# Other places in SBUF for the loads of the later retention, and another order of the steps, in a fused retention and SwiGLU kernel

## Chip, cores and metric

One core of a Trainium2 chip. The metric is the device time of one execution in microseconds (us); lower is better. "Span" is the stretch that the profiler shows of one execution, from its first instruction to its last.

## The reference

Retention with a decay per head is followed by a SwiGLU block. With batch 4, 8 heads, 768 positions and 64 numbers per head:

```python
for t in range(S):
    state = gamma[None, :, None, None] * state + np.einsum('bhd,bhe->bhde', k[:, :, t], v[:, :, t])
    y[:, :, t] = scale * np.einsum('bhd,bhde->bhe', q[:, :, t], state)
x = np.ascontiguousarray(y.transpose(0, 2, 1, 3)).reshape(B * S, H * D)   # 3072 x 512
g = x @ w_gate                                                             # 512 x 1536
silu = g * (1.0 / (1.0 + np.exp(-g)))
out = (silu * (x @ w_val)) @ w_out                                         # 1536 x 512
```

## The kernel before

The 3072 tokens are worked off in four segments of 6 x 128 tokens, 0 to 3. Each segment has a retention, which gives x; a pass up (gate and value products, silu, the product of both, giving h, kept in the tile `hT`, one row of 768 numbers per block `f` of 128 of the 1536 columns); and a pass down (h times `w_out`). The retention of segment s+1 is mixed into the end of the pass up and into the pass down of segment s, so that TensorE (PE) has work of the one while the other waits for vector work. Numbers are split in three parts before they meet PE (first part on ScalarE, ACT; second on VectorE, DVE; third on GpSimd, POOL, or on DVE).

Nothing schedules the program but a string, `PLAN`, of 2345 steps. The steps are recorded one by one in that order; each engine takes its own instructions in that order and waits at each for its operands and for its place to come free. So a step that waits holds up all that stands behind it on its engine. All loads and stores but a few go through one engine's queue, SP, and wait there in the same way: a load whose place is still being read holds up every later load.

Steps of segment s stand as `s/name`; those of the first pass up have no `s/`. The ones used below:

- `l0` to `l14` (`load_pair`): loads of the retention, 512 KB each; five for each of three pairs of chunks p: k and q turned (`l0 l1`, `l5 l6`, `l10 l11`, one DMA, L789), then v, k by rows, and q by rows (`l2 l3 l4`, `l7 l8 l9`, `l12 l13 l14`, four DMAs each, L793). The tuple `HOME` names for each load one of the `homes`, stretches of 1024 numbers per partition.
- `scp` scores on PE, `decp.i` decay on DVE (they free banks 4 to 7), `qp.c` scaling of q on DVE, `kp.n` scaling of k on ACT (L831), `Ap` and `Bp` the two halves of the mixing on PE (L798), `newp.z` the state on DVE (L897), `wasp.zg` and `mvp.z` on ACT (L889, L844), `yp.zr` y out of PSUM on ACT (L1025), `sum` and `x` the making of x (L414, L1003, L1010).
- `pf.n`: one of seven products of block f of a pass up (six matmuls, L1091). `uf.n`: silu and sums of that block on ACT and DVE. `wf.g.0`, `.1`, `.2`: the split of its weights (L994, L997, then L1000 on POOL or L414 on DVE; the set `ELSE` names those on DVE). `Lf` (`load_unit`, L1063): load of those weights, 896 KB, into `loads`, in which homes 0 to 4 lie too.
- `Df.t`: one step of a pass down (three matmuls, L1160), block f, 128 tokens t. `hf.0` to `.2`: split of row f of h. `Wf` (L1139; L1136 in segment 0): load of block f of `w_out`, 768 KB, into one of three slots; it waits until the last D of the block three before is done. In segment 0 it is 256 KB and is split by `df.0` to `.2` (ACT L1003, POOL or DVE, DVE), and `Zf` (L1150) stores the result.
- `et`, `ot`: result of tokens t out of PSUM into `chunk_x`, and its store (L1197). `Gf:i`, `Wf:i`, `if:i`, `jf:i`: the first pass up (PE, PE, ACT, DVE). `S`, `C`, `Z` of a number over 11: `w_out` as it is made in the first pass up.

Of the kernel before, what the change touches and what calls it, by code (L numbers as in the profile page):

```python
# [1331 lines left out]
```

## Time and profile before

| | us |
|---|---|
| three executions | 660.14, 662.2, 663.5 |
| median | 662.2 |
| the profiled execution | 666.25 |
| its span | 664.1 |

The page of the profile gives busy times by engine over the span and in 40 slices; the chain of waits follows the work that ended last back from the end; the timeline gives instructions of an engine in order of time, with the idle time before each in brackets and what ended it; the table by windows gives busy times and the granted clock of PE in chosen stretches. In the timeline "x33" is 33 instructions in a row that were merged. SPq is the SP queue; its column of time is the time to issue, not to land.

### The profile page before, as it was taken

The page shows a single profiled execution, that of the slowest core. Times are in us where ns is not written, and L with a number is a line of the kernel's source. Part 1 is how long each engine was busy: PE and PEld are TensorE (multiplying, and loading weights), DVE is VectorE, ACT ScalarE, POOL GpSimd, SP SyncE. Part 2 cuts the span into 40 slices and gives each one's busy share as a digit, 9 for nine tenths or more (in the row PEclk, how much of TensorE's full clock was granted, in tenths as well). Part 3 has the DMA queues.
Part 4 walks back from the last instruction along what each step waited for, and adds up shares of the span by engine and source line. Part 5 has one row for each costly group of instructions (what it writes and reads, how often), then busy time and mean ns, then how long its engine had stood idle before and what let it go on. Part 6 is the DMA issues. An engine that isn't in the chain of part 4 may idle for free.

```text
span 664.1 us, 14143 instructions
## 1 busy us (share of the span) xinstructions
PE 642.2 (97%) x5587; PEld 589.1 (89%) x5587; DVE 495.2 (75%) x760; ACT 391.7 (59%) x815; POOL 183.8 (28%) x122
## 2 busy tenths in 40 slices
PE   8999999998989989999999999999889999999997
PEld 7999989886869979998878999999678899999886
DVE  3988687867989947787689778787678788777541
ACT  3778788966655656556667665546474465554221
POOL 1442545420112745520000514520000524452000
PEclk9999999997999979999999999999899999999999
DMA  9899987897986651456884724446976643403564
GB/s 314 275 353 302 373 275 256 301 321 305 319 282 217 226 157 57 154 192 210 281 308 170 255 77 167 143 147 199 287 230 229 212 153 128 167 0 100 199 220 148
DMA packets 60850, 144.59 MB, mean 218 GB/s; under 512 B 5872, under 2 KB 33008, under 8 KB 60784
## 3 DMA queue, kind: packets, MB, share of 16 engines
q1 hardware_dynamic: 60208, 142.90, 63.3%
q8 instruction: 44, 0.72, 0.4%
q10 hardware_dynamic: 576, 0.79, 0.4%
q14 instruction: 22, 0.18, 0.1%
HBM read 113.78 MB, written 29.88 MB: 216 GB/s over the span
## 4 chain that ended last, share of the span: by engine, by line
PE 58%; DMA 4%; ACT 1%; SPq 0%; issue 0%; DVE 0%; ACTq 0%
PE bank L1091 35%; PE bank L1160 19%; DMA oitem<-wdnt 3%; PE bank L798 3%; DMA loads<-in_k_n_dram 0%; SPq L793 0%; ACT loads L831 0%; ACT states L889 0%; ACT gitem L994 0%; DVE chunk_x L1183 0%; ACT tmp L1106 0%; ACT bank L1107 0%; ACT chunk_x L1185 0%; ACT bank L1110 0%; ACT xb L1003 0%
## 5 line engine op out<-in xcount | busy, mean ns | idle before, releaser
L1160 PE MATMUL bank<-oitem,gitem 128*128 128x512 f32 x867 | 209.0, 398 | 6.2 <-DMA oitem<-wdnt 4.6
L1160 PEld LDWEIGHTS bank<-oitem,gitem 128*128 128x128 f32 x867 | 163.0, 191 | 43.0 <-DMA oitem<-wdnt 2.4
L1091 PE MATMUL bank<-xa,gitem 128*128 128x384 f32 x864 | 159.9, 339 | 3.3 <-ACT tmp L1106 3.3
L1091 PEld LDWEIGHTS bank<-xa,gitem 128*128 128x128 f32 x864 | 152.9, 191 | 4.0 <-ACT tmp L1106 3.6
L1000 POOL TENSOR_TENSOR gitem<-gitem 128x768 fp32r<-128x768 f32 x48 | 96.3, 2016 | 175.1 <-DVE gitem L997 154.0
L1000 POOL TENSOR_TENSOR oitem<-oitem 128x256 fp32r<-128x256 f32 (+1 forms) x51 | 56.1, 1103 | 167.8 <-DVE oitem L997 149.8
L922 PE MATMUL bank<-xa,oitem 128*128 128x384 f32 x480 | 85.3, 336 | 2.1 <-DVE hT L459 1.1
L922 PEld LDWEIGHTS bank<-xa,oitem 128*128 128x128 f32 x480 | 82.9, 188 | 3.6 <-DVE hT L459 1.8
L997 DVE SCALAR_TENSOR_TENSOR gitem<-gitem,loads 128x768 fp32r<-128x768 f32 x72 | 75.9, 1069 | 11.4 <-ACT gitem L994 11.3
L1091 PE MATMUL bank<-xb,gitem 128*128 128x384 f32 x432 | 81.8, 335 | 0.0
L994 ACT ACTIVATE gitem<-loads 128x768 fp32r<-128x768 f32 x72 | 58.8, 841 | 34.8 <-PE bank L1091 26.2
L1091 PEld LDWEIGHTS bank<-xb,gitem 128*128 128x128 f32 x432 | 75.8, 188 | 0.2
L414 DVE SCALAR_TENSOR_TENSOR gitem<-gitem 128x768 fp32r<-128x768 f32 x72 | 71.2, 994 | 1.9
L997 DVE SCALAR_TENSOR_TENSOR gitem<-gitem,hT 128x768 fp32r<-128x768 f32 x48 | 46.0, 962 | 23.3 <-ACT gitem L994 23.2
L994 ACT ACTIVATE gitem<-hT 128x768 fp32r<-128x768 f32 x48 | 39.9, 840 | 36.8 <-PE bank L1160 29.6
L1091 PE MATMUL bank<-xb,oitem 128*128 128x384 f32 x216 | 43.8, 337 | 0.0
L1108 DVE TENSOR_TENSOR hT<-bank,tmp 128x384 f32<-128x384 f32 x36 | 20.0, 555 | 30.6 <-PE bank L1091 29.9
L1107 ACT COPY tmp<-bank 128x384 f32<-128x384 f32 x36 | 17.2, 477 | 36.0 <-PE bank L1091 20.1
L1091 PEld LDWEIGHTS bank<-xb,oitem 128*128 128x128 f32 x216 | 38.0, 188 | 0.2
L889 ACT ACTIVATE states<-states,local 128x64 f32<-128x64 f32 x120 | 31.5, 335 | 1.5 <-DVE states L897 1.5
L1025 ACT COPY chunk_x<-bank 128x256 f32<-128x256 f32 x36 | 12.4, 367 | 30.4 <-DVE states L897 16.1
L1108 ACT COPY tmp<-bank 128x384 f32<-128x384 f32 x36 | 17.3, 480 | 14.1 <-PE bank L1091 14.0
(125 smaller groups left out, 786.2 us busy)
## 6 DMA issues: line engine op xcount, KB each, us to landing
loads<-wup SPq DMA_DIRECT2D x36, 896.0 KB, 5.0
oitem<-wdnt SPq DMA_DIRECT2D x33, 768.0 KB, 5.2
wdnt<-oitem SPq DMA_DIRECT2D x12, 768.0 KB, 5.3
wup<-first SPq DMA_DIRECT2D x9, 896.0 KB, 6.4
rawp<-in_w_gate_dram SPq DMA_DIRECT2D x12, 512.0 KB, 7.4
rawp<-in_w_val_dram SPq DMA_DIRECT2D x12, 512.0 KB, 6.5
rawp<-in_w_out_dram SPq DMA_DIRECT2D x12, 512.0 KB, 7.1
out_dram<-chunk_x SPq DMA_DIRECT2D x21, 256.0 KB, 2.3
```

Of the source, the lines that this page charges most:

```text
L414: stt(o, x, 1.0, y, op0=mul, op1=op)
L798: nc.tensor.matmul(o, a, b, start=start, stop=True, skip_group_check=True)
L889: act(states[:, z, g, n], states[:, 1 - z, g, n], AF.Copy, scale=lg[:, ds(NP * g + n, 1)])
L922: nc.tensor.matmul(o, w[:, a, ts(b, P)], X0[:, a, i, NC - 1 - b], start=a == b == 0, stop=a == 2 and b == NC - 1, skip_group_check=True)
L994: act(o[0], x, AF.Copy, scale=CUT / FAR)
L997: stt(o[1], f32(o[0]), -FAR, x, op0=mul, op1=add)
L1000: op(o[2], f32(o[0]), f32(o[1]), op=add)
L1025: copy(cx[:, ds(2 * r, 2), :, half[z]], y)
L1091: nc.tensor.matmul(o, w[:, a, k], x[:, a, KH - 1 - k], start=start and a == k == 0, stop=a == 2 and k == KH - 1, skip_group_check=True)
L1107: lambda: act(gate, c11, AF.Silu, scale=ONE), lambda: copy(u2, x),
L1108: lambda: copy(p5, wb), lambda: tt(h1, x, p5, op=add),
L1160: nc.tensor.matmul(banks[tok][:, cols], hs[f][:, a, ds(i * TH + u * P, P)], wo[f][:, a, cols], start=f == a == 0, stop=f == NF - 1 and a = ...
```

## The change

Before, the fifteen loads of a retention share seven homes: five in `loads`, the upper half of `chunk_x` and the second quarter of `tmp`. After, there are twelve: four more in the first 4096 numbers of `hT` (rows 0 to 5 of h, which are free once `h0` to `h5` have read them) and the lower half of `chunk_x` (free when the stores of the results of tokens 0, 1, 4 and 5 are done, and written by y later).

| load | before | after |
|---|---|---|
| l0, l1 (k, q of pair 0) | loads 2, loads 3 | chunk_x low, loads 2 |
| l2, l3, l4 | loads 4, chunk_x high, loads 2 | loads 3, chunk_x high, loads 4 |
| l5, l6 (pair 1) | loads 0, loads 1 | loads 2, chunk_x low |
| l7, l8, l9 | loads 3, tmp, loads 0 | tmp, hT 1, hT 0 |
| l10, l11 (pair 2) | loads 1, loads 4 | loads 0, loads 1 |
| l12, l13, l14 | chunk_x high, loads 0, loads 1 | hT 2, hT 3, chunk_x high |

The same 2345 steps are recorded, in another order from the 151st on, and `ELSE` has 50 names, not 45. In segment 0, `d0.1` and `e4` move to DVE and `d9.1` to POOL. Of the third parts of the weights of the passes up of segments 1, 2 and 3, 8, 13 and 12 stand on DVE before and 11, 11 and 16 after (the others on POOL); new on DVE in segment 1 are `w2.0.2`, `w2.1.2`, `w6.0.2`, `w7.2.2` and `w10.1.2`. Of the order, only the stretches that the prediction speaks of are shown.

```diff
     homes = [loads[:, ts(i, 1024)] for i in range(5)]
     homes += [chunk_x[:, ts(1, 1024)], tmp[:, ts(1, 1024)]]
-    HOME = (2, 3, 4, 5, 2, 0, 1, 3, 6, 0, 1, 4, 5, 0, 1)
+    homes += [hT.rearrange("p f i t -> p (f i t)")[:, ts(i, 1024)] for i in range(4)]
+    homes += [chunk_x[:, ts(0, 1024)]]
+    HOME = (11, 2, 3, 5, 4, 2, 11, 6, 8, 7, 0, 1, 9, 10, 5)
     blocks = [loads[:, ds(i, UNIT)] for i in (2048, 2048 + UNIT, 0)]
     lmask = local[:, : NP * HC].rearrange("p (i n) -> p i n", i=2)
...
-    G11:1 a17 b17 0/h1.0 1/k0.1 1/k0.3 0/W0 0/W1 j10:1 S17 c17 C17 0/h0.2
-    1/q0.1 1/was0.01 0/h1.1 j10:0 W11:0 i11:0 i11:1 1/l5 1/l6 0/d0.0 0/d0.1 j11:0 0/h1.2
-    Z17 0/h2.0 0/h4.0 0/d1.0 1/was0.00 0/d0.2 W11:1 0/W2 0/d1.1 j11:1 T10:1 0/Z0 1/A0
-    0/D0.0 0/d1.2 0/h2.1 0/D0.1 0/D0.2 1/sc1 1/l8 1/new0.0 0/h2.2 0/Z1 1/y0.00 0/d2.0 0/d2.1
-    1/mv0.0 1/dec1.1 1/dec1.0 1/was0.11 0/D0.3 0/D1.0 0/D0.4 0/D0.5 0/h3.0 1/l9 0/d2.2 0/Z2 1/k1.3
-    T9:2 T10:2 0/h4.1 0/D1.2 0/D1.3 0/D1.5 0/D1.1 0/h4.2 1/was0.10 1/y0.01 0/D1.4 1/k1.2 1/q1.0
-    0/h5.0 0/W3 0/d3.0 0/d3.1 1/k1.1 0/h3.1 1/q1.1 1/B0 0/D2.0 0/D2.1 0/D2.2 Z10 Z9
-    0/W4 1/begin 1/new0.1 0/d3.2 0/h5.1 0/h3.2 1/y0.10 1/y0.11 1/k1.0 1/mv0.1 0/D2.5 1/A1 0/D3.0
...
-    1/p2.3 1/u2.3 1/p2.4 1/w2.2.2 1/u2.4 0/e3 1/w3.2.1 1/w3.0.2 1/p2.5 1/u1.2 0/o3 1/u2.5 1/p2.6
-    1/L6 1/u0.7 1/u2.6 1/w4.1.0 1/w4.0.0 1/w4.2.1 1/w3.2.2 1/p3.0 1/w4.0.1 1/u2.8 2/l3 1/w5.2.0 1/w4.2.2
-    1/p3.1 1/w4.1.1 1/w4.0.2 1/u3.0 1/p3.2 1/u3.1 1/L7 1/p3.3 1/u3.3 1/u2.2 1/u2.7 1/p3.4 1/u3.4
-    1/w4.1.2 2/k0.3 1/u1.7 1/p3.5 1/w5.1.0 1/w5.0.0 1/u3.5 1/u2.9 1/p3.6 1/w6.2.0 1/w5.2.1 1/w5.2.2 0/e5
...
-    1/D5.5 1/D4.4 1/D5.0 1/D5.4 2/l13 2/y1.11 2/was1.11 2/y1.10 2/sum1.2 2/x1.1.0 2/new1.1 2/mv1.1 1/D5.3
-    2/L0 1/W7 1/D5.2 1/D6.0 2/sc2 2/x1.1.2 2/sum1.0 2/sum1.1 2/sum1.3 1/W8 1/h7.0 1/h7.1 1/h7.2
...
-    2/h1.1 2/u11.3 2/u11.2 2/u11.4 2/p11.4 2/u11.5 3/l8 2/p11.5 2/h2.0 2/h1.2 2/D0.0 2/u11.6 2/D0.2
-    2/p11.6 3/begin 2/u11.7 2/h2.1 2/u11.8 2/h4.0 2/u11.9 2/D0.1 2/D0.3 2/D1.0 3/k1.3 3/k1.1 3/k1.2
-    3/k1.0 2/h2.2 2/h4.1 2/h4.2 3/A0 3/new0.0 3/was0.10 3/sc1 3/y0.01 3/y0.00 2/D1.3 2/D1.1 3/l9
-    2/W2 3/was0.11 3/dec1.1 2/D1.2 3/mv0.0 3/dec1.0 2/D0.4 2/D0.5 2/D1.5 2/W3 2/h3.0 3/B0 3/y0.10
...
-    2/h5.1 2/h5.2 2/h6.1 2/D4.1 2/D3.0 2/W6 3/A1 3/new1.0 3/x0.0.1 2/h6.2 2/D4.0 3/y1.00 3/y1.01
-    2/D4.2 2/D4.3 3/mv1.0 3/was1.10 3/was1.11 3/B1 3/l13 3/new1.1 3/y1.10 3/y1.11 3/x0.0.2 3/sum1.0 3/sum1.1
-    3/sum1.3 2/D4.4 2/D4.5 3/L0 2/W7 2/h7.0 3/sc2 3/was2.01 3/x1.2.0 3/x1.2.1 3/dec2.0 2/h7.1 3/k2.3
...
+    c17 0/h1.0 1/k0.1 i11:0 G11:1 i11:1 0/W0 1/k0.3 0/d0.0 1/cm j10:1 0/h0.2 1/q0.0
+    Z11 1/q0.1 0/W1 j10:0 W11:0 S17 C17 0/h1.1 1/l9 1/was0.01 0/h1.2 W11:1 Z17
+    0/h2.0 0/d1.0 0/h4.0 1/was0.00 0/W2 j11:0 j11:1 1/l7 0/d0.1 0/d0.2 0/Z0 1/A0 0/h2.1
+    1/new0.0 T10:1 1/mv0.0 1/l8 0/D0.0 1/sc1 0/D0.1 1/y0.00 0/d2.0 0/d1.1 0/d2.1 0/d1.2 0/Z1
+    1/was0.11 0/D0.3 0/D0.2 0/D1.1 0/D1.0 1/dec1.1 1/dec1.0 0/D0.4 0/D0.5 0/D1.2 0/D1.3 0/h3.0 0/d2.2
+    0/Z2 0/h4.1 T9:2 T10:2 0/h2.2 0/D1.5 1/y0.01 1/k1.3 0/W3 1/B0 0/D1.4 0/D2.2 1/k1.2
+    1/was0.10 1/q1.0 0/h5.0 0/d3.0 0/h3.1 Z10 0/h4.2 1/new0.1 1/q1.1 0/D2.0 0/D2.1 Z9 0/W4
+    1/begin 0/h5.1 0/d3.1 0/d3.2 1/l10 0/Z3 0/h3.2 1/y0.10 1/y0.11 1/k1.1 1/mv0.1 0/D2.3 1/k1.0
+    1/A1 0/D3.0 1/x0.1.0 0/d4.0 1/was1.00 1/x0.1.2 1/sum0.0 1/sum0.1 1/l12 0/D2.5 0/D2.4 0/h6.0 0/W5
...
+    1/u0.9 1/p2.1 1/p2.0 1/w2.1.1 1/w2.2.1 1/w2.2.2 0/e3 0/o3 0/o1 1/L5 1/u1.4 1/w3.1.0 1/w3.1.1
+    2/l3 1/u1.5 1/w2.1.2 1/p1.5 1/w3.0.0 1/u2.0 1/w3.2.0 1/u1.6 1/w1.2.2 1/p1.6 1/u1.8 1/w4.2.0 1/w3.2.1
+    1/u2.1 1/w3.1.2 1/p2.2 1/w3.0.1 1/u1.9 1/p2.3 1/u2.3 1/p2.4 1/u2.4 1/p2.5 1/w3.0.2 1/w3.2.2 1/u1.2
+    1/u2.5 1/p2.6 1/L6 1/u2.6 1/w4.2.1 1/w4.1.0 1/w4.0.0 1/w4.1.1 1/w4.0.1 1/w4.0.2 1/p3.0 1/u2.8 1/w5.2.0
+    1/p3.1 1/u3.0 1/p3.2 1/u0.7 1/L7 1/p3.3 1/u3.3 1/u2.2 1/u2.7 1/p3.4 1/u3.4 1/w4.1.2 1/w4.2.2
+    2/k0.3 1/u1.7 1/p3.5 1/w5.1.0 1/w5.0.0 1/u3.5 1/p3.6 1/u2.9 1/u3.8 1/w6.2.0 1/w5.2.1 1/w5.2.2 0/e5
...
+    1/u11.5 2/q0.1 1/w11.2.2 1/p11.6 2/begin 1/u11.6 1/u11.7 1/h2.1 2/l8 1/W2 1/D0.1 1/D0.3 1/D0.0
+    1/u11.8 1/u11.9 2/A0 2/sc1 2/y0.00 2/k1.1 1/h2.2 2/l10 1/h4.1 2/l7 1/D1.0 1/D1.3 1/D0.2
+    2/k1.0 2/y0.01 2/k1.3 2/dec1.0 2/dec1.1 1/h4.2 1/D0.4 1/D0.5 1/W3 1/D1.5 1/h3.0 1/D1.1 1/D1.2
+    1/D1.4 1/W4 1/h5.0 2/new0.0 2/mv0.0 1/h3.1 2/q1.0 1/D2.1 1/D2.5 2/was0.10 2/k1.2 2/B0 2/L0
+    1/D2.2 1/D2.4 2/q1.1 1/h5.1 2/was0.11 2/y0.11 2/new0.1 2/mv0.1 1/h3.2 1/h5.2 2/was1.00 2/was1.01 2/y0.10
+    2/x0.2.0 2/sum0.2 2/sum0.0 2/sum0.1 2/x0.1.0 2/x0.1.1 2/sum0.3 2/x0.2.1 2/x0.1.2 1/D2.0 1/D2.3 1/W5 1/h6.0
+    1/h6.1 1/h6.2 2/l12 2/x0.0.0 2/l13 1/D3.3 1/D3.2 1/D4.3 1/D3.5 2/L1 1/D3.4 1/D3.1 1/D3.0
+    1/W6 2/x0.0.2 2/A1 2/y1.00 2/new1.0 2/was1.10 2/x0.2.2 1/D4.1 2/x0.0.1 2/y1.01 1/D5.1 1/D4.0 1/D4.5
...
+    2/p11.1 3/q0.0 3/q0.1 2/u10.6 2/u9.7 2/h1.1 2/h0.1 3/l9 2/u11.1 2/u10.9 2/p11.2 2/u10.7 2/p11.3
+    2/u11.3 2/p11.4 2/u11.2 2/u11.4 2/p11.5 2/h2.0 2/h0.2 2/u11.5 3/l7 2/h1.2 2/p11.6 2/u11.8 2/D0.0
+    2/D1.0 2/u11.6 2/u11.7 2/D0.2 3/begin 2/h4.0 2/u11.9 2/h2.1 3/l8 2/D0.3 3/k1.2 3/k1.1 2/h2.2
+    3/sc1 2/h4.1 2/h4.2 3/dec1.0 3/A0 3/new0.0 3/y0.01 3/y0.00 3/was0.10 2/D0.1 2/D1.1 2/D1.3 3/mv0.0
+    3/k1.0 3/was0.11 3/dec1.1 2/D0.4 2/D0.5 2/h3.0 2/D1.2 2/h3.1 3/q1.0 2/h3.2 2/D1.5 2/W2 2/W3
+    2/D1.4 2/W4 2/h5.0 3/B0 3/k1.3 3/y0.10 3/l12 2/D2.3 2/D2.0 3/l10 2/D2.1 2/D2.2 2/D2.4
...
+    3/x0.1.2 3/x0.2.2 3/was1.01 3/sum0.0 3/sum0.1 3/mv0.1 2/D3.2 3/A1 3/was1.00 3/new1.0 3/x0.2.1 3/sum0.3 2/h5.1
+    3/L0 3/l13 2/h5.2 2/D3.3 2/D4.2 2/D3.0 2/W6 2/D4.0 2/D4.1 3/y1.00 2/h6.0 3/y1.01 3/x0.0.0
+    3/mv1.0 3/B1 3/was1.11 3/was1.10 3/new1.1 2/h6.1 2/h6.2 3/y1.10 3/y1.11 2/D4.4 3/x0.0.1 3/x0.0.2 3/sum1.0
+    3/x1.2.0 3/x1.2.2 3/sum1.1 3/was2.01 2/D4.5 2/D4.3 2/W7 3/was2.00 3/k2.0 2/D5.2 2/D5.1 2/D5.0 2/D5.3
+    3/sc2 2/D5.4 2/D5.5 3/k2.1 2/h7.0 2/h8.0 2/h7.1 2/h8.1 3/x1.1.0 2/h9.0 3/dec2.0 3/sum1.3 3/k2.2
```

## The prediction

> **What bounds the kernel now.** I read the page first: the span and the busy times.
>
> ```profile
> span 664.1 us, 14143 instructions
> PE 642.2 (97%) x5587; PEld 589.1 (89%) x5587; DVE 495.2 (75%) x760; ACT 391.7 (59%) x815; POOL 183.8 (28%) x122
> ```
>
> PE is the bound, and the change gives it no instruction more or fewer. What can move is its idle time, 664.1 - 642.2 = 21.9 us with both ends, and time that it runs at a lower clock. So the timeline of PE comes next, for each place in the span at which PE stood, then the windows around the longest.
>
> ```profile
> 132.10 4.43 PE L922 MATMUL bank<-xa,oitem 128*128 128x384 f32 x24 [1.12 <-DVE hT L459]
> 154.98 0.90 PE L798 MATMUL bank<-tmp,loads 64*64 64x64 f32 x29 [1.89 <-ACT chunk_x L1025]
> 195.90 0.96 PE L798 MATMUL bank<-tab,chunk_x 64*64 64x64 f32 x29 [1.30 <-DVE states L897]
> 242.40 7.04 PE L1091 MATMUL bank<-xa,gitem 128*128 128x384 f32 x24 [3.31 <-ACT tmp L1106]
> 252.40 4.33 PE L1091 MATMUL bank<-xa,gitem 128*128 128x384 f32 x24
> 340.52 5.04 PE L1160 MATMUL bank<-oitem,gitem 128*128 128x512 f32 x21 [1.20 <-ACT states L889]
> 469.86 10.72 PE L1160 MATMUL bank<-oitem,gitem 128*128 128x512 f32 x39 [1.99 <-DMA oitem<-wdnt]
> 488.58 7.77 PE L1160 MATMUL bank<-oitem,gitem 128*128 128x512 f32 x33
> 498.31 3.00 PE L1160 MATMUL bank<-oitem,gitem 128*128 128x512 f32 x12 [1.96 <-DMA oitem<-wdnt]
> 517.37 6.40 PE L1160 MATMUL bank<-oitem,gitem 128*128 128x512 f32 x27 [0.69 <-DMA oitem<-wdnt]
> ```
>
> The bracket is PE's idle time. Equal rows give the price of the clock: 24 matmuls took 7.04 after the wait of 3.31 and 4.33 ten microseconds later, 2.7 more; 39 down matmuls took 10.72 after the wait of 1.99, where 33 took 7.77, that is 39 in 9.2, so 1.5 more. In the table by windows the last three figures are PE's clock, the DMA share and GB/s:
>
> ```profile
> 153.00:163.00 10.00, 7.93 (x108) 6.38 (x108) 5.93 (x12) 7.41 (x22) 1.26 (x1) 0.66 0.70 282
> 239.00:249.00 10.00, 6.69 (x24) 6.61 (x24) 3.28 (x6) 6.63 (x17) 4.19 (x2) 0.66 0.27 105
> 467.00:477.00 10.00, 8.01 (x27) 6.20 (x28) 8.09 (x16) 7.25 (x17) 0.00 (x0) 0.83 1.00 310
> 496.00:506.00 10.00, 8.04 (x135) 6.09 (x136) 8.67 (x12) 4.90 (x10) 0.00 (x0) 1.00 0.89 283
> ```
>
> After the waits of 1.89, 3.31 and 1.99 the clock fell, by 3.4, 3.4 and 1.7 us of full-clock work in ten; after that of 1.96 it did not. A wait near 2 us may thus cost itself or nearly twice itself. The Trainium skill ("TensorE: Matmul & The Clock Gate", Part 1 and the goals under "Why this matters for your kernels") states that the clock halves after an idle window of about 3.4 us, that the window runs freely, and that gaps up to about 3 us are safe. This trace disagrees on the last: 1.89 and 1.99 were enough. By the page's rule only the wait of 3.31 has a clock price, and the sum below would be 1.5 us smaller.
>
> **Part by part.** From the rows above a D step is 7.77 / 11 = 0.71 us and a product 4.33 / 4 = 1.08; scores and mixing come from these rows (64 and 96 matmuls). The distances below are counted in `PLAN` with these four prices.
>
> ```profile
> 140.41 1.16 PE L798 MATMUL bank<-loads 64*64 64x64 f32 x64
> 328.74 1.56 PE bank L798 x96
> ```
>
> *Pass up 1, the wait of 3.31.* ACT waits here for l3:
>
> ```profile
> 228.53 2.97 SPq L793 DMA_DIRECT2D chunk_x<-in_k_n_dram  x4
> 237.69 0.40 ACT L831 ACTIVATE chunk_x<-chunk_x,local 128x128 f32<-128x128 f32 x1 [3.33 <-DMA chunk_x<-in_k_n_dram]
> 238.98 0.40 ACT L831 ACTIVATE chunk_x<-chunk_x,local 128x128 f32<-128x128 f32 x1 [0.89 <-DMA chunk_x<-in_k_n_dram]
> ```
>
> From the first issue, 228.53, to the second half's arrival, 238.98, are 10.5 us. `PLAN` puts four products (p3.1 to p3.4, 4.3 us) between `2/l3` and `2/k0.3`; silu and sums queue behind k0.3, and PE runs dry. After, twelve stand there (p1.5 to p3.4, 13.0 us), and l3 still stands right behind `o3`. 13.0 covers 10.5, so the wait and its slow matmuls go: -3.3 - 2.7 = -6.0. What would be late next on ACT is work for products a unit further on.
>
> *Pass down 2, the waits of 1.99 and 1.96.* The queue of SP:
>
> ```profile
> 461.03 2.73 SPq L793 DMA_DIRECT2D loads<-in_q_t_dram  x4
> 463.86 5.95 DMA oitem<-wdnt
> 488.19 0.54 SPq L1063 DMA_DIRECT2D loads<-wup  x1
> 488.82 9.35 DMA oitem<-wdnt
> 510.60 6.64 DMA oitem<-wdnt
> oitem<-wdnt SPq DMA_DIRECT2D x33, 768.0 KB, 5.2
> ```
>
> Here `3/l9` wanted the home of l5, held until sc1; its four issues (2.73) stood ahead of W2, which landed 5.95 after its issue and 2 us late. After, l9 and l7 issue well before; ahead of W2 stands l8, held by `h2.1`. From there to D2.1 PE has nine D steps, sc1, A0 and B0: 6.4 + 1.2 + 3.1 = 10.7 against 2.7 + 6.0 = 8.7. The wait goes with its clock: -3.5. W7 landed after 9.35 because l13 and L0 (896 KB) went out just before it, all held by B1. After, L0 needs only B0 and l13 only `h5.1`: both stand ahead of W6, eight D steps and B1 (7.2) before W7, which then has twelve D steps and sc2 (9.7) to land, against the usual 5.2: -2.0. W10 keeps its eight D steps (5.7 against 6.64), so the 0.69 stays.
>
> *Pass down 1, the wait of 1.20.* In the chain of waits, the way to this one runs from l13 (home of l9, held by B1) over the scaling of k on ACT to PE. After, l13 is in `hT`, held by `h5.1`, some 18 us of PE ahead of k2.1: -1.2.
>
> *Pass down 0.* W11:0 waited 1.12 for `j10:0`, on DVE behind `S17` and `h1.1`; after, both stand behind it: -1.1. But `d0.1`, now DVE's, and `d0.2` stand behind `j11:1`, which can't start before the last matmul ahead of A0 is done. These rows stand for the three:
>
> ```profile
> L459 DVE TENSOR_TENSOR hT<-bank,tmp 128x384 f32<-128x384 f32 x20 | 10.9, 551 | 6.2 <-ACT tmp L459 3.7 <-PE bank L922 2.5
> L1010 DVE SCALAR_TENSOR_TENSOR oitem<-oitem 128x512 fp32r<-128x512 f32 x12 | 8.2, 686 | 5.4 <-POOL oitem L1006 5.3
> ```
>
> 0.55 + 2 x 0.69 = 1.9 with some 0.2 of latency, against 1.56 of A0, then D0.0 needs them: +0.6. The wait of 1.89 at A1 came from W3 by way of d3.0 and y0.1:
>
> ```profile
> 142.89 3.50 SPq L793 DMA_DIRECT2D loads<-in_q_t_dram  x4
> 147.12 0.38 SPq L1136 DMA_DIRECT2D oitem<-wdn  x1
> 153.46 0.63 ACT L1003 ACTIVATE oitem<-oitem 128x512 fp32r<-128x512 f32 x1 [3.87 <-DMA oitem<-wdn]
> ```
>
> W3 stands behind Z2, so behind d2.0 to d2.2, so behind the landing of W2. After, l9's four issues (3.50 as here) stand ahead of W2, and I put W2 1.3 late; against that W3 to A1 holds one D step more (0.7), a scaling of k has left ACT's queue ahead of y0.1 (0.7), and D0.0 already lost 0.6. 1.89 + 1.3 - 0.7 - 0.7 - 0.6 = 1.2, between 0 and 4: I leave this wait and its clock as they are, 0. The 1.30 at B2 and the smaller ones stay too: DVE is as loaded in this stretch as before.
>
> *New waits.* In passes 1 and 2, l8 now waits for `h2.1`, and k1.1 or k1.2 on ACT for l8; two y, one was and mv0.0 queue behind, and B0 needs them.
>
> ```profile
> loads<-in_k_n_dram SPq DMA_DIRECT2D x12, 128.0 KB, 2.9
> L831 ACT ACTIVATE chunk_x<-chunk_x,local 128x128 f32<-128x128 f32 x24 | 8.1, 392 | 4.7 <-DMA chunk_x<-in_k_n_dram 4.7
> L889 ACT ACTIVATE states<-states,local 128x64 f32<-128x64 f32 x120 | 31.5, 335 | 1.5 <-DVE states L897 1.5
> L1025 ACT COPY chunk_x<-bank 128x256 f32<-128x256 f32 x36 | 12.4, 367 | 30.4 <-DVE states L897 16.1 <-PE bank L798 12.9 <-DVE xb L414 1.3
> ```
>
> Issue and landing 2.7 + 2.9; on ACT two k of two instructions (1.6), two y (0.7), a was of four at 31.5 / 120 (1.1) and mv0.0, taken like two y (0.7): 9.7 from `h2.1` to B0, where PE has nine D steps, sc1 and A0, 9.2. So 0.5 late in each pass: +1.0. In pass 1, W2 has 0.4 to spare (twelve D steps, A0 and sc1, 11.2, against the end of h2.1, 2.1 after p11.6, and 8.7), and W5, queued behind L0, has eight D steps and A1 (7.2) against 5.2 to 9.35, so 0 to 2.1 late: +0.5. Nothing that reads a home was seen late for the two loads in `chunk_x` low; if the cover of o5 went, l0 has 37 us in pass 1. Moved DMAs are the same bytes; passes 3 and the first up are taken as before.
>
> Sum: -6.0 - 3.5 - 2.0 - 1.2 - 1.1 + 0.6 + 1.0 + 0.5 = -11.7, from the profiled execution's 666.25 (span 664.1 and 2.15 outside) to 654.5. That execution lies 4.05 over the median of 662.2, so an ordinary one may hold one slow-clock stretch less, and there is about 2 less to win: 662.2 - 11.7 + 2 = 652.5.
>
> **Rivals.** *Slower: DVE bounds pass up 1.* Today's first half of that pass:
>
> ```profile
> 208.00:239.00 31.00, 31.00 (x179) 30.77 (x178) 24.71 (x39) 15.77 (x33) 19.88 (x12) 1.00 0.63 196
> L414 DVE SCALAR_TENSOR_TENSOR gitem<-gitem 128x768 fp32r<-128x768 f32 x72 | 71.2, 994 | 1.9
> L414 DVE SCALAR_TENSOR_TENSOR xa<-xa,tmp 128x1024 fp32r<-128x1024 f32 x9 | 11.0, 1218 | 0.0
> ```
>
> DVE (third busy figure) has 24.7 of 31. After, w2.0.2 and w2.1.2 (2.0), x2.0.1 (1.2), now behind p0.0, and e4 (0.7, as the 128x512 above) come on top: 28.6, and 2.4 of idle are left for its waits, not 6.3. If it needs the 20% that it has now, 28.6 becomes 35.9, 4.9 late, and another such loss in the second half, where w6.0.2 and w7.2.2 join; broken into four waits over 2 us with a slow clock of 1.7 each, 9.8 + 6.8 over 652.5 is 669. It decides once DVE needs more than 2.4. Against it: weights are split a unit ahead.
>
> *Given back.* The four-part loads in front of W2 and W5 in pass 1, or of W3 in pass 0, cost two waits of 2 with 2.5 of clock each: 652.5 + 9 = 661.5.
>
> *The homes do not decide.* W loads wait for their slots anyway, and new holds (`h2.1`, `h5.1`) take the place of B0 and B1; only pass up 1 and W11:0 improve: 662.2 - 7.1 + 2.1 = 657.
>
> *More than forecast.* The wait at A1 goes as well, with 3.4 of clock, and no new ones come: 652.5 - 1.9 - 3.4 - 1.5 = 645.7.
>
> **How the numbers follow.** Forecast 0.54, more 0.10, homes do not decide 0.14, given back 0.13, slower 0.09. Differences under 0.5% (3.3 us: under 658.9 is faster, over 665.5 slower) a measurement of this kernel can hardly tell from none. Faster 0.54 + 0.10 + 0.14 = 0.78; same 0.13; slower 0.09. The forecast's own spread, from the waits at A1 (0 to 4) and W5 (0 to 2.1) and the clock, is some 5 to each side; the range reaches past "more" to 644 and past "given back" to 663, leaving out the slower case and some of the tails.
>
> **What the profile after would show.** Right: no wait for `in_k_n` on L831 in pass up 1 and no slow clock there; no PE wait on `oitem<-wdnt` over 1 us in pass 2; l9 and L0 issued earlier; the wait at A1 still there; 0.7 at W10. Wrong: waits of 2 us on DVE's hT lines in pass up 1; W2 or W5 late in pass 1; more than three slow-clock stretches.

## The result and the profile after

| | executions (us) | median | ratio to before | profiled execution | its span |
|---|---|---|---|---|---|
| before | 657.98 to 663.5 (5) | 660.14 | | 666.25 | 664.1 |
| after | 648.92 to 653.76 (5) | 650.1 | 0.9851, 95% [0.9803, 0.9899] | 648.92 | 647.1 |

The executions of before are those taken beside the changed kernel; with the ratio, the 662.2 of the prediction becomes 652.3 (649.2 to 655.5 by the interval), where 652.5 was forecast. The way there was partly another one. The page of after, its span, its busy times and the line of PE's clock in 40 slices:

```profile
span 647.1 us, 14096 instructions
PE 633.4 (98%) x5587; PEld 581.1 (90%) x5587; DVE 503.2 (78%) x763; ACT 392.8 (61%) x817; POOL 184.2 (28%) x117
PEclk9999999999999999999999999999999999999999
```

The same 5587 matmuls are busy 8.8 us less: no slice is below full clock. The other 8.2 of the 17.0 us between the two spans were idle time. The timeline of PE in after, at the places the prediction named (the bracket is the idle time before the row):

```profile
153.25 0.90 PE L801 MATMUL bank<-tmp 64*64 64x64 f32 x29 [0.67 <-ACT chunk_x L1028]
166.73 0.63 PE L801 MATMUL bank<-tmp 64*64 64x64 f32 x27 [1.02 <-ACT chunk_x L1028]
235.54 4.32 PE L1094 MATMUL bank<-xa,gitem 128*128 128x384 f32 x24
317.56 2.79 PE L1163 MATMUL bank<-oitem,gitem 128*128 128x512 f32 x11 [0.67 <-DMA oitem<-wdnt]
500.48 6.37 PE L1163 MATMUL bank<-oitem,gitem 128*128 128x512 f32 x27 [0.26 <-DMA oitem<-wdnt]
```

A1 of pass down 0 waits 0.67, not 1.89. Pass up 1 has no wait: 24 matmuls take 4.32 where they took 7.04. W10 in pass down 2 is 0.26 late, not 0.69. New are 1.02 at B1 and 0.67 at W5 of pass down 1. The same four windows as before (the last three figures are PE's clock, the DMA share and GB/s):

```profile
150.00:160.00 10.00, 9.02 (x124) 7.08 (x123) 5.24 (x9) 5.16 (x13) 1.27 (x1) 1.00 0.99 386
239.00:249.00 10.00, 10.00 (x59) 10.00 (x59) 8.79 (x15) 6.43 (x12) 3.62 (x2) 1.00 0.52 203
467.00:477.00 10.00, 10.00 (x192) 8.10 (x191) 7.33 (x11) 8.83 (x28) 0.00 (x0) 1.00 1.04 348
496.00:506.00 10.00, 9.74 (x43) 7.79 (x42) 8.27 (x11) 3.69 (x7) 1.83 (x1) 1.00 0.50 152
```

The stretch around A1 now runs at full clock (0.66 before), which was not forecast. Last the groups by line. First the down matmuls, before and after (busy time, mean ns of one, then idle time ahead of them and its releasers):

```profile
L1160 PE MATMUL bank<-oitem,gitem 128*128 128x512 f32 x867 | 209.0, 398 | 6.2 <-DMA oitem<-wdnt 4.6 <-ACT states L889 1.2 <-DVE tmp L820 0.4
L1163 PE MATMUL bank<-oitem,gitem 128*128 128x512 f32 x867 | 205.1, 393 | 1.6 <-DMA oitem<-wdnt 0.9 <-DVE oitem L1013 0.4 <-POOL oitem L1009 0.3
```

Waits for `w_out` fell from 4.6 to 0.9 us. And the scaling of k on ACT in after:

```profile
L834 ACT ACTIVATE chunk_x<-chunk_x,local 128x128 f32<-128x128 f32 x24 | 8.1, 395 | 0.0
L834 ACT ACTIVATE hT<-hT,local 128x128 f32<-128x128 f32 x48 | 16.3, 391 | 9.5 <-DMA hT<-in_k_n_dram 9.5
```

ACT no longer waits for l3, which lies in `chunk_x` (4.7 before). It does wait 9.5 us for k in `hT`, all but 0.6 of it at k1.x for l8, as the prediction said, but PE waits nowhere for that.

### The profile page after: what moved, and what is told of

Same layout as the page of the kernel before. It is cut to its first block, busy times and chain, and to the rows that moved or that the text cites. A ratio compares the mean times of both kernels' runs of the same rounds, so it can differ in the third digit from the quotient of the medians.

```text
span 647.1 us, 14096 instructions
## 1 busy us (share of the span) xinstructions
PE 633.4 (98%) x5587; PEld 581.1 (90%) x5587; DVE 503.2 (78%) x763; ACT 392.8 (61%) x817; POOL 184.2 (28%) x117
## 4 chain that ended last, share of the span: by engine, by line
PE 74%; DMA 14%; DVE 5%; ACT 4%; issue 2%; SPq 1%; POOL 1%; ACTq 0%; DVEq 0%
PE bank L1094 41%; PE bank L1163 24%; PE bank L801 4%; PE bank L943 3%; DMA oitem<-wdnt 2%; DMA rawp<-in_w_gate_dram 2%; DMA hT<-in_v_n_dram 2%; DMA oitem<-wdn 2%; DMA rawp<-in_w_out_dram 2%; DMA chunk_x<-in_k_n_dram 1%; DMA wup<-first 1%; DMA wdnt<-oitem 1%; DVE oitem L1000 1%; DMA wdn<-first 1%; DVE first L415 1%
## 5 line engine op out<-in xcount | busy, mean ns | idle before, releaser
L1163 PE MATMUL bank<-oitem,gitem 128*128 128x512 f32 x867 | 205.1, 393 | 1.6 <-DMA oitem<-wdnt 0.9
L1163 PEld LDWEIGHTS bank<-oitem,gitem 128*128 128x128 f32 x867 | 160.4, 188 | 37.6 <-DVE oitem L1013 1.4
L1003 POOL TENSOR_TENSOR gitem<-gitem 128x768 fp32r<-128x768 f32 x49 | 98.0, 2009 | 261.0 <-DVE gitem L1000 240.8
L1094 PE MATMUL bank<-xa,gitem 128*128 128x384 f32 x864 | 156.5, 334 | 0.0
L1094 PEld LDWEIGHTS bank<-xa,gitem 128*128 128x128 f32 x864 | 150.4, 188 | 0.3
L1000 DVE SCALAR_TENSOR_TENSOR gitem<-gitem,loads 128x768 fp32r<-128x768 f32 x72 | 70.4, 990 | 9.2 <-ACT gitem L997 9.0
L1003 POOL TENSOR_TENSOR oitem<-oitem 128x512 fp32r<-128x512 f32 (+1 forms) x45 | 54.5, 1216 | 67.3 <-DVE oitem L1000 59.1
L1110 ACT COPY tmp<-bank 128x384 f32<-128x384 f32 x36 | 17.2, 479 | 40.1 <-PE bank L1094 25.0
L1000 DVE SCALAR_TENSOR_TENSOR oitem<-oitem,loads 128x256 fp32r<-128x256 f32 (+1 forms) x42 | 27.6, 657 | 6.1 <-ACT oitem L997 6.1
L550 ACT ACTIVATE first<-rawp 128x1024 f32<-128x1024 f32 (+1 forms) x17 | 17.6, 1033 | 16.5 <-DMA rawp<-in_w_gate_dram 9.5
```

Source lines behind the costliest of these rows:

```text
L550: act(d, hi.bitcast(F32), AF.Copy, scale=2.0 ** -112)
L1000: stt(o[1], f32(o[0]), -FAR, x, op0=mul, op1=add)
L1003: op(o[2], f32(o[0]), f32(o[1]), op=add)
L1094: nc.tensor.matmul(o, w[:, a, k], x[:, a, KH - 1 - k], start=start and a == k == 0, stop=a == 2 and k == KH - 1, skip_group_check=True)
L1163: nc.tensor.matmul(banks[tok][:, cols], hs[f][:, a, ds(i * TH + u * P, P)], wo[f][:, a, cols], start=f == a == 0, stop=f == NF - 1 and a = ...
```

## The experiments

All ratios are to the kernel before, run beside each; 0.001 is 0.66 us. The changed kernel's is 0.985. What the change consists of was taken apart first: places (`HOME`), order (`PLAN`), and the set of third parts on DVE (`ELSE`). The new order with places and set both old was not run; e1 has the new set with it.

| kernel | places | order | set | ratio, 95% |
|---|---|---|---|---|
| e2b | new | old | old | 1.0052 [1.0029, 1.0075] |
| e10 | old | old | new | 1.0095 [1.0060, 1.0130] |
| e1 | old | new | new | 1.0281 [1.0250, 1.0312] |
| e8 | new | new | old | 0.9961 [0.9935, 0.9987] |
| after | new | new | new | 0.9851 [0.9803, 0.9899] |

**e1, the order without the places.** Against after:

```diff
-    HOME = (11, 2, 3, 5, 4, 2, 11, 6, 8, 7, 0, 1, 9, 10, 5)
+    HOME = (2, 3, 4, 5, 2, 0, 1, 3, 6, 0, 1, 4, 5, 0, 1)
```

and 23 loads behind the last reader of their place (`2/l0` by 116 steps, behind `1/w9.0.1`).

> The changed order and set of third parts, with the old seven places; 23 loads stand later, each right behind the last reader of its place. Theory (the twelve places make the early loads possible, and the early loads take W2's, W7's and l13's waits away; the change of order in the pass up takes the wait at k0.3 away): pass up 1 stays clean, since l3 keeps its place (no wait over 1 us on the scaling of k at 235 to 245, no half clock there), but loads wait for places again: waits of 1 to 3 us on PE in the passes down of segments 1 and 2, some with half clock behind them; time 653 to 659, of which 6 us under the kernel before are the pass up. Rival (the order alone does it, the places do not decide, since the W loads wait for their slots anyway): within 0.3% of the changed kernel's 650, no PE wait over 1 us in the passes down. Second rival (places are worth more than I think): 662 or above, since the order was made for twelve places.

680.23 us: of the three only the second rival, 662 or above, holds, and by far. The timeline of PE in e1, one step of its chain of waits, and its group of down matmuls:

```profile
157.07 1.30 PE L801 MATMUL bank<-tmp,loads 64*64 64x64 f32 x29 [3.84 <-ACT chunk_x L1028]
282.70 1.75 PE L801 MATMUL bank<-loads 64*64 64x64 f32 x64 [4.67 <-DMA loads<-in_q_t_dram]
278.57 4.00 DMA loads<-in_q_t_dram
354.72 5.26 PE L1163 MATMUL bank<-oitem,gitem 128*128 128x512 f32 x15 [5.39 <-DMA oitem<-wdnt]
L1163 PE MATMUL bank<-oitem,gitem 128*128 128x512 f32 x867 | 212.1, 401 | 10.7 <-DMA oitem<-wdnt 9.1 <-DVE oitem L1013 0.8 <-DVE gitem L415 0.6
```

Pass up 1 has no wait at k0.3, as the theory said. But with seven places the first scores wait for a load (4.67, and 3.90 a segment later) that gets its place only at 278.57, when PE is already idle, and W waits grow to 9.1 us. So the rival "the homes do not decide" is refuted: this order can't stand without them.

**e2 and e2b, the places in the old order.** Against before, `HOME` and the list `homes` as in after; moved behind the last reader of their new place are `2/l8`, `3/l7`, `3/l8`, `3/l12`. In e2 one load, `1/l7`, goes into `tmp` while the last silu of segment 0 still needs that place, so that part of h is spoiled; in e2b it stands behind `j11:1`.

> The twelve places with the order of before; only four loads (l8 in pass 1, l7, l8, l12 in pass 2) stand later, behind the last reader of their new place. Theory: the order in pass up 1 is the old one, four products between l3 and k0.3, so its wait of 3.3 and its half clock stay; a load that stands at its old step is issued at its old step or a little earlier, so W2 and W7 in pass 2 gain at most part of their 3.5 and 2.0, and l13's 1.2 in pass down 1 goes; time 655 to 661 against 660 to 662 of before. Rival (the places alone do it): 652 or less, W2's and W7's waits under 0.7. Rival (the places alone hurt, new holds by h in front of the queue): 663 or more.

> As e2 (twelve places, the order of before), with l7 of the first later segment also behind the last reader of its new place in tmp. Theory (the places take the waits for W2 and W7 away in the old order too, but the wait at k0.3 stays): within 0.3% of e2's 660.3; no PE wait over 1 us on w_out in the pass down of segment 2, a wait of 1.8 to 3.3 at 238 to 243. Rival (e2's time came from its one load that stood too early): 663 or more, or under 657.

e2 took 660.3 us, 0.9970 [0.9938, 1.0001]. e2b took 664.79: its rival's bound of 663 was passed, so e2's time did hang on the load that stood too early, and I keep to e2b. With it the last rival of e2 holds (the places alone hurt, 663 or more). In e2b, by group and timeline:

```profile
L1156 PE MATMUL bank<-oitem,gitem 128*128 128x512 f32 x867 | 205.9, 394 | 3.4 <-DVE oitem L1006 2.0 <-DMA oitem<-wdnt 1.4
L827 ACT ACTIVATE hT<-hT,local 128x128 f32<-128x128 f32 x48 | 16.1, 391 | 13.7 <-DMA hT<-in_k_n_dram 13.7
240.74 4.63 PE L1087 MATMUL bank<-xa,gitem 128*128 128x384 f32 x16 [2.75 <-ACT tmp L1102]
313.51 0.63 PE L794 MATMUL bank<-tab,loads 64*64 64x64 f32 x27 [1.23 <-ACT chunk_x L1021]
```

The places alone do what the theory says of W: 4.6 us of waits become 1.4. The wait in pass up 1 stays. And the new wait of the prediction appears: k1.x on ACT waits for l8 in `hT` (13.7 us in all), y queues behind it, and B0 waits 1.23 in pass 1, 1.64 and 1.23 in passes 0 and 2. The old order pays for the places with that; in the new one, with the k moved, it does not reach PE.

**e3, only the step of pass up 1.** Against before:

```diff
 1/p3.4 1/u3.4 1/w4.1.2
-2/k0.3
...
 1/p4.5
+2/k0.3 2/k0.1 2/k0.0 2/k0.2
```

`2/k0.1`, `2/k0.0` and `2/k0.2`, which stood up to three products ahead of that place, go along.

> The kernel before with the four scalings of k of segment 2 in pass up 1 moved back from four products behind the load l3 to twelve. Theory (ACT waits for l3 with silu queued behind it, and the wait of 3.3 brings 2.7 of slow clock): no PE wait over 1 us at 235 to 245 and no half clock there, 3.3 to 6 us off, 655 to 658 with the rest unchanged. Rival (the wait moves on, because DVE, busy 25 of 31 us there, or the first scores of segment 2 are next late): PE waits of 2 to 3 us elsewhere in pass up 1 or at the scores, time within 0.3% of before.

658.05 us, 0.9949 [0.9926, 0.9972]: 3.4 us off, the lower end of what was expected. In e3 ACT takes the eight instructions of k at 241.55 with no wait ahead of them, and PE has none above 0.4 in the pass:

```profile
241.55 2.44 ACT L831 ACTIVATE chunk_x<-chunk_x,local 128x128 f32<-128x128 f32 x8
335.80 1.38 PE L1160 MATMUL bank<-oitem,gitem 128*128 128x512 f32 x5 [1.67 <-DMA oitem<-wdnt]
```

The second row is a wait for `w_out` behind the edit, where before had 1.20 for the state: some of the gain is given back there, but hardly more than 0.5, since e4, which up to there is the same program as before, waits 1.46 for `w_out` at this place.

A lag can be read off two profiles of kernels that give PE the same matmuls in the same order: the start of each matmul in the one, less its start in the other. By this PE in e3 gains 6.2 us on before at k0.3, what the prediction has for this step. By 350 us it has given back 2.1: 0.9 in the same pass, the rest at 317 and at the wait above.

**e5, the same step undone in the changed kernel.**

```diff
 1/u1.9 1/p2.3
+2/k0.3
...
-2/k0.3
 1/u1.7 1/p3.5
```

> The changed kernel with one step moved back: k0.3 of segment 2 stands four products behind the load l3, as before, not twelve. Theory (ACT waits there for the load's second half, with silu and sums queued behind it): ACT idle for some 5 us ahead of this k0.3, a PE wait of 3 to 3.5 in pass up 1 with one or two stretches of 3.4 us at half clock, 3.3 to 6 us slower than the changed kernel: 653 to 656. Rival (in the changed kernel other work covers it, as DVE has its third parts spread otherwise): no wait over 1.5, 650 to 651.

657.05 us, 0.9925 [0.9899, 0.9950], a microsecond above what was expected, and by the ratios some 5 us over after (the intervals just touch, so 3.6 to each side). The mechanism is back as described:

```profile
226.82 0.40 ACT L834 ACTIVATE chunk_x<-chunk_x,local 128x128 f32<-128x128 f32 x1 [2.90 <-DMA chunk_x<-in_k_n_dram]
228.39 3.42 PE L1094 MATMUL bank<-xa,gitem 128*128 128x384 f32 x12 [3.19 <-ACT tmp L1110]
```

ACT's idle time was 2.90, not 5, since it reached k0.3 3.9 us behind l3's first issue. PE lost 3.19, and the next 12 matmuls took 3.42 instead of 2.2. By the lag, PE in e5 loses 5.0 us on after here and gets back 1.0 at W5 of pass down 1, where it no longer waits.

**e4, only W2 of pass down 2.** Against before:

```diff
-3/l9 2/W2
+2/W2 3/l9
```

> The kernel before with the load l9 of segment 3 moved from just ahead of W2 of segment 2 to just behind it; nothing else. Theory (l9 waits for its place and its four issues hold W2 up in the SP queue): W2 issues some 2.7 us earlier, the wait of 1.99 at 468 goes with its stretch of half clock, 2 to 3.5 us off, 657 to 660. Rival (W2 waits for its slot, not for l9): issue and wait unchanged, time unchanged. Rival (l9 now late itself): a wait of 1 to 3 on k of the second chunk in its place, time unchanged.

659.94 us, 0.9973 [0.9952, 0.9994]: 1.8 us off, with 0.4 to 3.2 in the interval. In e4's SP queue W2 now goes out at 454.89, ahead of l9's four issues, and its wait is gone; the wait at W7 stays:

```profile
454.89 0.53 SPq L1139 DMA_DIRECT2D oitem<-wdnt  x1
459.23 2.63 SPq L793 DMA_DIRECT2D loads<-in_q_t_dram  x4
492.91 2.32 PE L1160 MATMUL bank<-oitem,gitem 128*128 128x512 f32 x9 [2.18 <-DMA oitem<-wdnt]
```

l9 itself went out 4.3 us later than W2 could: what held W2 up before was l9's own wait for its place, not only its 2.7 of issues. 2.18 is the wait at W7 (1.96 in the profile of before), whose loads still stand ahead.

**e8, the old set in the changed kernel.** Against after, `ELSE` of before (45 names).

> The changed kernel with the old set of third parts (45 names on DVE, not 50). The rival of the prediction that ended slower (DVE bounds pass up 1 because of the five third parts and e4 that move to it) would make this faster than the changed kernel by 1 us or more, 646 to 649. Theory (DVE had room, and the parts were moved because POOL was late with them): PE waits of 0.5 to 1.5 on third parts out of POOL at some of the moved names, 650.5 to 654; d0.1 on POOL again costs up to 0.6 at D0.0 and a split of W in segment 0 is late.

658.59 us: by the two ratios 7.3 us of the change (3.6 to each side) hang on this set, more than the theory gave, and the opposite of the rival that put DVE's load as the danger. PE in e8's pass up 1, POOL there, and after's groups of a third part on POOL and of such a part on DVE:

```profile
218.49 2.22 PE L1087 MATMUL bank<-xa,gitem 128*128 128x384 f32 x8 [3.23 <-POOL gitem L996]
214.08 4.35 POOL L996 TENSOR_TENSOR gitem<-gitem 128x768 fp32r<-128x768 f32 x2 [7.09 <-DVE gitem L993]
L1003 POOL TENSOR_TENSOR gitem<-gitem 128x768 fp32r<-128x768 f32 x49 | 98.0, 2009 | 261.0 <-DVE gitem L1000 240.8 <-PE bank L1094 11.4 <-ACT tmp L1111 8.8
L415 DVE SCALAR_TENSOR_TENSOR gitem<-gitem 128x768 fp32r<-128x768 f32 x71 | 71.1, 1006 | 1.6
```

Two parts in a row on POOL take 4.35 us, and PE waits 3.23 for the second; a stretch of half clock follows. By the lag PE in e8 loses 5.1 us on after here, of 8.2 between the two profiles; the rest is spread over short waits. One such part costs 2.01 us on POOL and 1.01 on DVE. The Trainium skill ("GPSIMD Engine Reference", section 4.1, Engine selection) gives two-input elementwise work on GpSimd about twice VectorE's time; these rows agree.

**e10, the new set alone.** Against before, `ELSE` of after (50 names).

> The kernel before with the changed set of third parts (50 names on DVE, not 45), places and order as before. Theory after the runs so far (the set belongs to the order: in the changed order the old set costs some 8 us, in one POOL wait of 3.2 and others): in the old order the new set is worth nothing or loses, 661 to 668, with new PE waits of 1 to 3 us on third parts in the passes up. Rival (the set gains by itself, and the places and the order gain the rest): 652 to 657.

668.48 us, just past the upper end of what was expected: it loses by itself. Two of its longest waits of PE:

```profile
166.14 2.15 PE L1154 MATMUL bank<-oitem,gitem 128*128 128x512 f32 x6 [1.86 <-DVE oitem L1004]
244.94 1.43 PE L1085 MATMUL bank<-xa,gitem 128*128 128x384 f32 x5 [2.39 <-ACT tmp L1100]
```

The first is in pass down 0, behind a split of W on DVE; at the same matmul e3 and e4, with the old set, wait 1.04 and 0.94 and before not at all, so at most part of it is the set's. The second is the old wait of pass up 1. The theory's waits of 1 to 3 on third parts in the passes up were not there: apart from that row the longest wait in the passes up of segments 1 to 3 is 0.94. The loss is spread over many short waits, 21.2 us in sum against 17.3, and their whole cause isn't settled.

**e9 and e6, what took A1's wait away.** Against after, `0/W2` behind `1/l7` (e9), and `1/l5`, `1/l6` behind `1/l9` (e6):

```diff
-0/W2 j11:0 j11:1 1/l7
+j11:0 j11:1 1/l7 0/W2
```

> The changed kernel with W2 of segment 0 moved behind l7, nothing else: four issues of l7 (some 3.4 us) go out ahead of it. Theory (the wait at A1 in pass down 0 hangs on W2 through d2, the store Z2 and the issue of W3, so an earlier W2 took it from 1.89 to 0.67): W2 issues at 140 and lands at 143 to 145, W3 lands 2 to 3 us later than 152.3, the wait at A1 is 2 to 3.5 with a stretch of half clock behind it: 652 to 656. Rival (the order of the steps on ACT ahead of A1 did it): W3 later, but the wait at A1 under 1, 650 to 651.

> The changed kernel with l5 and l6 of segment 1 moved to just behind l9, so that all three go out ahead of W2, as l5 and l6 did before. Theory (what took the wait at A1 in pass 0 from 1.89 to 0.67 is that W2 landed 4.6 us after its issue instead of 6.5, because l5 and l6 no longer load beside it): W2 takes 6 to 7 us to land, W3 follows, the wait at A1 is 1.7 to 3 again, with a half-clock stretch behind it in most executions: 652 to 655. Rival (the order of the steps on ACT and PE ahead of A1 did it): W2 late, wait at A1 under 1, 650 to 651.

e9 took 651.31 us, 0.9836 [0.9794, 0.9877]. ACT and PE in e9:

```profile
154.18 0.63 ACT L1006 ACTIVATE oitem<-oitem 128x512 fp32r<-128x512 f32 x1 [1.55 <-DMA oitem<-wdn]
155.12 0.90 PE L801 MATMUL bank<-tmp 64*64 64x64 f32 x29 [1.63 <-ACT chunk_x L1028]
```

W2 went out at 141.4, W3 landed 1.9 later than in after, and A1's wait rose from 0.67 to 1.63, less than the 2 to 3.5 expected, with a stretch of half clock behind it. So W2's arrival does set A1's wait. The time did not follow: by the lag, PE in e9 loses 2.4 us on after at A1 and gets back 1.4, at B1 (0.44 for 1.02) and at W5 (whose 0.67 went). In e6, 651.15 us, 0.9838 [0.9807, 0.9868], W2 took 7.9 us to land, more than the 6 to 7 expected, but another wait came first:

```profile
145.47 1.97 PE L801 MATMUL bank<-chunk_x,loads 64*64 64x64 f32 x64 [3.40 <-DMA chunk_x<-in_q_t_dram]
```

sc1 waited 3.40 for l6, and behind it A1 waited no more. By the lag PE in e6 loses 5.0 us on after at sc1 and has made up all of it by W5 of pass down 1: 2.1 up to the end of A1, 1.6 by B1, 0.9 at W5, the rest at short waits. Neither kernel can be told from the changed one by its time, whose interval is 3.2 us to each side, so what A1's wait is worth in time stays open.

**e7 and e7b, the remaining waits mended.** Against after: `j7:0` ahead of `S10`; `1/y0.10 1/y0.11 1/k1.1` ahead of `0/d3.0`; `1/y1.01` (in e7b `1/mv1.0` as well) ahead of `0/d5.0`; `2/l12` ahead of `2/L0`; in e7 also `1/sc0` behind `G10:0`. There l6 takes l0's place ahead of sc0, so the first scores of segment 1 are spoiled in e7.

> The changed kernel with its five longest waits mended, each by moving steps of one engine past a step that waits: j7:0 ahead of S10 (the 1.01 at 107), sc0 behind G10:0 (the 0.68 at 119), y0.10, y0.11 and k1.1 ahead of d3.0 (the 0.67 at 153), y1.01 ahead of d5.0 (the 1.02 at 166), l12 of segment 2 ahead of L0 (the 0.67 at 317). Theory (each wait has its own cause on the queue of one engine, and what is late next is 0.3 to 0.5 later): 2 to 4 us off, 646 to 648.5, no PE wait over 0.6 behind the first 20 us. Rival (each is given back one step later): 649.5 to 651.

> The changed kernel with four of its waits mended: j7:0 ahead of S10 (the 1.01 at 107), y0.10, y0.11 and k1.1 ahead of d3.0 (the 0.67 at 153), y1.01 and mv1.0 ahead of d5.0 (the 1.02 at 166), l12 of segment 2 ahead of L0 (the 0.67 at 317); sc0 stays where the changed kernel has it, ahead of l6, which takes its place. Theory (each of these waits has its cause on the queue of one engine): 2 to 3.4 us off the changed kernel's 650.1, 646.7 to 648.5; no PE wait over 0.7 behind the first 20 us. Rival (each is given back one step later): 649.5 to 651.

e7: 654.9 us, 0.9893 [0.9860, 0.9925], slower than either forecast: G10:0 waits 1.95 ahead of the scores, with a stretch of half clock behind it, and by the lag (but for sc0, e7 has after's order on PE) PE is 0.3 us behind after's ahead of this place, 3.6 behind it and 4.2 at the end. e7b: 651.43 us, 0.9837 [0.9788, 0.9887], no better than after. The rival was right that nothing is gained, as the timeline of PE in e7b shows:

```profile
103.67 0.96 PE L925 MATMUL bank<-xa,oitem 128*128 128x384 f32 x4 [1.37 <-ACT tmp L460]
120.84 1.16 PE L801 MATMUL bank<-loads,chunk_x 64*64 64x64 f32 x64 [1.35 <-DVE loads L571]
317.44 2.79 PE L1163 MATMUL bank<-oitem,gitem 128*128 128x512 f32 x11 [1.22 <-DMA oitem<-wdnt]
480.02 3.26 PE L1163 MATMUL bank<-oitem,gitem 128*128 128x512 f32 x13 [1.25 <-DMA oitem<-wdnt]
```

The waits at 107, 153 and 166 are gone; the fourth, at 317, has grown from 0.67 to 1.22. New or longer are 1.37 at 102, 1.35 for 0.68 at sc0, and a W wait of 1.25 at 479.

## Why the prediction was right, step by step

| step | forecast | profile after | runs |
|---|---|---|---|
| pass up 1, k0.3 | -6.0 | wait and slow clock gone | alone -3.4 (e3), undone about +5 (e5) |
| W2, pass down 2 | -3.5 | gone | alone -1.8 (e4) |
| W7, pass down 2 | -2.0 | gone | gone in e2b |
| l13, pass down 1 | -1.2 | gone | gone in e2b |
| W11:0 | -1.1 | gone | 0.70 to 1.55 in every kernel with the old order, 0.14 at most with the new |
| D0.0 | +0.6 | 0.22 | |
| k1.x to B0, passes 1 and 2 | +1.0 | no wait | waits of 1.23 in each (e2b, old order) |
| W5, pass down 1 | +0.5 | 0.67 | |
| A1, pass down 0 | 0 | -1.2, and 3.4 of clock | e9: hangs on W2 |
| B2, pass down 0 | 0 | 0.17, so -1.1 | |
| new: B1, j7:0, sc0 | not seen | 1.02, 1.01, 0.68 | |

Five steps went as worked out, in sign and in mechanism. For pass up 1 and W2 the runs bear that out one by one; W7 and l13 go with the places (e2b) and W11:0 with the order, but what each is worth in time was not measured.

**The step that failed is A1.** I put W2 1.3 us late, for l9's issues ahead of it, and left the wait as it was. W2 went out at the same time in both (136.56 and 136.57) and landed 2.0 earlier, 4.55 us after its issue instead of 6.54: before, l5 and l6 had gone out just ahead of it, and I counted issues but not what else is in flight. e6 bears that out: with l5 and l6 ahead again W2 takes 7.9. The issues, and ACT's first work on W2 (d2.0), four rows of before and two of after:

```profile
134.41 0.38 SPq L789 DMA_DIRECT2D loads<-in_k_t_dram  x1
134.85 0.46 SPq L789 DMA_DIRECT2D loads<-in_q_t_dram  x1
136.56 0.32 SPq L1136 DMA_DIRECT2D oitem<-wdn  x1
143.12 0.63 ACT L1003 ACTIVATE oitem<-oitem 128x512 fp32r<-128x512 f32 x1 [1.65 <-DMA oitem<-wdn]
136.57 0.40 SPq L1139 DMA_DIRECT2D oitem<-wdn  x1
141.15 0.63 ACT L1006 ACTIVATE oitem<-oitem 128x512 fp32r<-128x512 f32 x1
```

W3 landed 1.1 earlier, ACT was 0.6 quicker from d3.0 to y, PE came 0.5 earlier: 1.89 - 1.1 - 0.6 + 0.5 = 0.7. A wait of 0.67 brought no slow clock. That is the rival "more than forecast", of which this half came true.

**The new wait at B0 (+1.0) did not come.** I had mv0.0 end on ACT 9.7 us behind h2.1 and B0 wait for it. In pass 2 of after it ends 9.4 behind, at 456.06; but B0 starts at 455.60 without a wait, since its first matmuls don't read what mv0.0 writes. The first that does starts at 456.23.

**Two terms were too large for an ordinary execution.** One minus the mean granted clock, times the span, gives what an execution lost to the half clock: 3.2 us on average for before (0.9952 over 86 executions), where the profiled one (0.987) lost 8.6, and 0.9 for after's five (1.0, 0.997, 1.0, 1.0, 0.996). So some 2.3 of the 10 us are clock and the rest waits. For k0.3 the 2.7 of clock was about right, and the wait was not: in e3 (0.9982, so 1.9 of clock gained) 1.5 of its 3.3 came through, in e5 (0.9938, 3.1 lost) some 2. These are differences of medians, with 1.5 and 3.6 us to each side, but the lags agree: the whole 6.2 is gained at k0.3 in e3, and 2.1 is given back further on. For W2 it was the other way: e4's 1.8 is nearly the whole wait of 2.0, and its clock (0.9954) is no better than before's, so the 1.5 of clock does not show.

**That the total came out right is in part luck.** With its correction of 2 the forecast holds 7.5 us of waits and 2.2 of clock; measured are 7.7 and 2.3. But in the profiles A1 and B2, left at nothing, bring 2.3 and the B0 wait, put at a loss of 1.0, costs nothing, while the waits at B1, j7:0 and sc0, which I did not see, take 2.7. And the correction stood for one stretch of half clock, where the profiled execution had lost 5.4 us more than an ordinary one.

**What I did not see at all is the set of third parts.** I treated it only as a load on DVE, as the rival that ends slower. DVE has 25.7 busy of the 31 us of pass up 1, not 28.6, and no wait there:

```profile
208.00:239.00 31.00, 31.00 (x180) 30.83 (x179) 25.71 (x44) 20.36 (x44) 14.73 (x11) 1.00 0.67 219
```

The other side is that with the old set POOL, with its double time, is late in the new order; the whole set is worth some 7 us there (e8). Of the rival "given back" only short waits came, 0.67 at W5 and 0.67 at A1. The prediction came out of waits taken one at a time, and the runs show that the three parts of this change don't add up: each of those tried alone, places and set, loses 0.5 to 1%, order with set loses 2.8%, and together they win 1.5%.

## What to carry to other kernels

In a program ordered by hand, places, order and split of work between engines are one thing: a change of one that loses alone may be what makes another pay, so it is tried with the steps behind it reordered. Waits are priced by what comes next: in e7b three were taken away, a fourth grew and others came up, for no gain; in e6 PE fell 5.0 us behind at one wait and had made it up 180 us later. For a load, count what is in flight beside it, not only what is issued ahead of it.

## What the runs showed of the clock

PE's clock in the records changes only at the edges of windows of 3.41 us, whose grid lies otherwise in each execution. In these profiles what goes with a fall is how much of one such window PE is idle. Windows of before (first figure after the length is PE's busy time, the third from the end the clock):

```profile
466.50:469.92 3.42, 1.43 (x37) 0.88 (x28) 2.56 (x5) 1.57 (x3) 0.00 (x0) 1.00 0.93 367
469.92:473.33 3.41, 3.41 (x8) 2.75 (x9) 3.13 (x8) 2.85 (x10) 0.00 (x0) 0.50 1.12 247
493.81:497.22 3.41, 2.54 (x12) 1.76 (x10) 2.71 (x5) 3.34 (x11) 0.00 (x0) 1.00 0.96 247
497.22:500.64 3.42, 2.33 (x10) 1.97 (x11) 2.42 (x4) 2.29 (x3) 0.00 (x0) 1.00 1.04 270
```

The wait of 1.99 fell whole into one window, and the next ran at half clock. The wait of 1.96 lay across an edge, 0.87 and 1.09, and nothing followed. This answers what the prediction left open there. Now a wait of 1.67 inside one window of e3, behind which the clock stayed, and one of 1.84 inside one window of e2, behind which it fell:

```profile
333.01:336.42 3.41, 1.74 (x8) 1.14 (x8) 3.18 (x5) 2.87 (x9) 0.00 (x0) 1.00 1.01 408
336.42:339.83 3.41, 3.41 (x17) 2.83 (x16) 0.63 (x2) 1.48 (x2) 0.00 (x0) 1.00 1.12 280
238.11:241.52 3.41, 1.57 (x10) 1.33 (x9) 2.76 (x4) 3.20 (x9) 1.75 (x1) 1.00 0.06 23
241.52:244.93 3.41, 3.41 (x12) 3.41 (x12) 0.00 (x0) 1.94 (x5) 2.47 (x2) 0.50 0.77 269
```

Over all fourteen profiles, each of the 21 full-clock windows with 1.84 us idle or more was followed by one at half clock, none with under 1.40 was; in between it was 4 of 13, all four with 64x64 matmuls of the mixing in them (and so had one of the other nine). At half clock, the four windows with 0.77 or more idle kept it there, and of those with less only two, both full of mixing. So in these runs a wait of 1.84 us or more that fell whole into one window cost clock. A wait of twice that must fill 1.84 of some window wherever it lies; between these it is chance, which differs from execution to execution and should make part of their spread. The Trainium skill ("TensorE: Matmul & The Clock Gate", Part 1) has the free-running window of 3413 ns, which these traces confirm, but has the clock fall after an idle window of that length; here a little over half of one was enough.
